# Half of a first MLP layer as seven Strassen block products, with token sums on GpSimd, in a fused window attention and MLP kernel

## The chip, the cores and the metric

One core of a Trainium2 chip runs the whole program; the other cores stay idle. The metric is device microseconds of one execution, the median of several runs; lower is better. Engines are named as in the profile: PE (TensorE, matmuls; PEld are its weight loads), DVE (VectorE), ACT (ScalarE), POOL (GpSimd), SP (SyncE, here a DMA queue).

## The reference

Attention over 4 batches, 8 heads, 768 tokens and 64 dimensions, where each query sees the last 128 tokens and the first 4; then a layer norm, an MLP of 512 to 2048 to 512 with ReLU, and a residual sum:

```python
scores = scale * np.matmul(q, k.transpose(0, 1, 3, 2))
keep = is_sink | in_window            # pos < 4, or 0 <= rel < 128
a = softmax(np.where(keep, scores, -1e9))
x = concat_heads(np.matmul(a, v))     # (4, 768, 512)
mu, var = mean(x), var(x)             # over the 512 features
xn = (x - mu) / np.sqrt(var + 1e-06) * g_ln
out = x + np.maximum(xn @ w_ch1, 0.0) @ w_ch2
```

## The kernel before

The 3072 tokens are 24 tiles of 128, taken two at a time: 12 chunks of 256 tokens, three per batch. All matmul operands are bf16, sums are fp32 in PSUM.

**Attention of a chunk** (`chunk`, `attend`, `value`). q and k are loaded by GpSimd's DMA queue into `nat` tiles (L659), transposed by DMA on SP's queue (L551) into `kq`; v goes into `vn` (L562). Scores are made in two halves (PE, L763, with four small matmuls for the sink tokens, L767), exponentiated on ScalarE (L777) and masked on VectorE (L781, two bf16 tensors in SBUF). For each of the two tiles, `value` multiplies with v (L800, L805) into a PSUM pair; VectorE takes the reciprocal of the row sum (L818), writes x (L820), its statistics (L824, L826); GpSimd takes the inverse root (L832, L833); VectorE writes the centred and scaled x (L835, `xc`), and SP transposes it by DMA into `xnt`, the right operand of the MLP.

**MLP of a chunk** (`mlp`, `wino`). The first layer is eight units of 8 matmuls of 256 columns (L880): unit u gives two of the 16 blocks of 128 hidden features, in one PSUM bank; ScalarE applies the ReLU on the way into `hq` (L890). From chunk 2 on the second layer is a Strassen product in Winograd's form (`wino`): VectorE makes eight sums of hidden blocks (`hs`, L943: s1 to s4, each for two halves g), PE makes seven products p1 to p7 of 8 matmuls of 256 columns (L960) in three banks, and VectorE drains them with the residual (`tm`, L974) and into the output tile (`ot`, L981). p6 adds onto p1's bank region after p1 was copied by L974, p4 and p5 onto others likewise. The sums of the weight blocks are made once (L1029). Chunks 0 and 1 make the first layer by tile, in matmuls of 128 columns (L873), and have a plain second layer (L911).

**What sets the order.** Nothing is issued in the order of the source. Every operation is registered in a `Plan` with a priority, the engines that may run it and a duration; `Plan.run` simulates the engines, picks the ready operation of the lowest priority number, and the program is emitted in that order; each engine then executes its own list strictly in that order. The attention of chunk c+1 (`value`) falls between the units of chunk c's MLP, and the scores of chunk c+2 between the second-layer products of chunk c. Buffers are taken from rings (`P.ring`) with a fixed number of slots; PSUM has two pairs (attention) and four single banks `one` (everything else). Priorities are 16 per chunk (`T`, `at`) plus offsets from the dictionary `PAR`.

Of the kernel before, what the change touches and what calls it, by code (L numbers as in the profile page):

```python
# [7 lines left out]
FP32 = mybir.dt.float32  # L8
BF16 = mybir.dt.bfloat16
AF = mybir.ActivationFunctionType  # L10
ALU = mybir.AluOpType
# [198 lines left out]


def fix(occ, extra=0.09):
    return (occ, occ + extra)
# [13 lines left out]
NEVER = -1e9  # L227

PAR = dict(split=(3, 4, 5, 6, 7), gsum=-8.0, guard=183.0, strict=40.0, win=0.4, tr=-8.0, sc=-5.3, sc1=-2.0, av=2.0, trx=9.0, by_dma=4, x_by_dma=2, g_on_w=2, av2=20.0, avi=1.0, behind=5, gtt=9.0, ramp=0.3, vs0=2.6, vpb=12.0,
           w1p=(0.15, 1.7, 2.05, 2.8), pm=2, w2p=(4.5, 4.51, 4.52, 4.53), by_tile=2, wino=2, vp=(0.0, 0.1, 2.0, 2.1, 4.2, 4.3), ld1=0.05)  # L230


def general(tc, nc, slots, pairs, ones, ident_f, ident, w1, w2, mhalf, g_s, g_r, q, k, v, out, scale):
# [128 lines left out]
def kernel(  # L362
# [34 lines left out]
    def ring(name, n, shape, dtype, pool=consts):  # L397
        P.ring(name, [Slot(pool.tile(shape, dtype, name=f"{name}{i}"), f"{name}{i}") for i in range(n)])
# [8 lines left out]
    ring("nat", 8, [128, H, 64], BF16)  # L407
    ring("vn", 7, [128, H, 65], BF16)
    ring("kq", 4, [128, HP, 2, 256], BF16)
    ring("pe", 12, [128, 2, 512], BF16)  # L410
    ring("ps", 3, [128, 256], BF16)
    ring("kts", 2, [128, HP, 32], BF16)
    ring("x", 16, [128, DM], BF16)
    ring("xc", 6, [128, DM], BF16)
    ring("xnt", 4, [128, NDM, 256], BF16)
    ring("hq", 8, [128, 4, 512], BF16)
    ring("hs", 10, [128, 2, 2, 128], BF16)
    ring("tm", 6, [128, 256], FP32)
    ring("ot", 4, [128, DM], FP32)
    ring("st", 16, [128, 24], FP32)  # L420
# [317 lines left out]
    def attend(c):  # L738
# [48 lines left out]
        for i in range(2):  # L787
            def part(h, n, i=i):
                col = 256 * i + 128 * n if R else 128 * (i + n)
                return pes[h // 2].t[:, h % 2, col:col + 128]  # L790
            value(c, i, pes, ps, (PAR["av2"] if c == 2 else at(c, "av")) + PAR["avi"] * i, part, [2 * c + i - 1, 2 * c + i] if R or i else [2 * c])

    def value(c, i, pes, ps, d, part, srcs):
        b, R, t = c // RC, c % RC, 2 * c + i
# [2 lines left out]
        def av(e):  # L797
# [5 lines left out]
            for h in range(H):  # L803
# [14 lines left out]
        P.op(f"rc{t}", {"DVE": fix(0.115)}, d + 0.1, lambda e: V.reciprocal(rc(), pv()[:, :, :, 64]),  # L818
             reads=[po], writes=[rcb])
        P.op(f"x{t}", {"DVE": dve(512)}, d + 0.11, lambda e: V.tensor_tensor(  # L820
            x.t.rearrange("p (a h c) -> p a h c", a=2, c=64), pv()[:, :, :, 0:64],
            rc().unsqueeze(3).to_broadcast([128, 2, 4, 64]), op=ALU.mult), reads=[po, rcb], writes=[x])
        mv = Buf(f"mv{t}")
        P.op(f"bn{t}", {"DVE": fix(0.60)}, d + 0.12, lambda e: V.bn_stats(st.t[:, 8:14], x.t),  # L824
             reads=[x], writes=[st, mv])
        P.op(f"ag{t}", {"DVE": fix(0.09)}, d + 0.13, lambda e: V.bn_aggr(st.t[:, 14:16], st.t[:, 8:14]),  # L826
             reads=[st], rw=[mv])
        rs = Buf(f"rs{t}")
        xst_b[t, "rs"] = rs
        scaled = c >= PAR["wino"]  # L830
        roots[t] = P.op(f"rs{t}", {"POOL": (0.83, 0.88)}, d + (0.5 if scaled else 5), lambda e: (
            G.tensor_scalar(st.t[:, 17:18], st.t[:, 15:16], 1e-6, None, op0=ALU.add),  # L832
            G.tensor_tensor(st.t[:, 16:17], st.t[:, 17:18], mhalf, op=ALU.pow)),  # L833
            reads=[st, mv, Bc["mhalf"]], writes=[rs])
        P.op(f"xc{t}", {"DVE": fix(0.26)}, d + (0.6 if scaled else 0.14), lambda e: V.tensor_scalar(  # L835
            xc.t, x.t, st.t[:, 14:15], st.t[:, 16:17] if scaled else None, op0=ALU.subtract,
            **({"op1": ALU.mult} if scaled else {})), reads=[x, st, mv] + ([rs] if scaled else []), writes=[xc])
        pt = Buf(f"ptx{t}", "one")
# [14 lines left out]
        if c >= PAR["g_on_w"]:  # L853
# [4 lines left out]
            [nc.scalar.mul(dst()[:, j], src()[:, j], gt[:, j:j + 1]) for j in range(NDM)]),  # L858
            reads=[pt, Bc["gt"]], writes=[xnt_b[c], xnt_t[t]])

    def mlp(c):
        T = 16.0 * c + 8.0
        xnt = xnt_b[c]
        h1 = []
        by_tile = c < PAR["by_tile"]
        hq = [Buf(f"hq{c}_{g}", "hq") for g in range(2)]
        for u in range(NH1 // 2):
            ph, hb, hg = Buf(f"ph{c}_{u}", "one"), Buf(f"h{c}_{u}"), hq[u // 4]

            def mm_t(e, u=u, ph=ph):  # L870
                for s in range(4):
                    for j in range(NDM):
                        nc.tensor.matmul(ph.t[:, 128 * s:128 * s + 128], lhsT=w1[u // 2][:, j, 128 * s:128 * s + 128],  # L873
                                         rhs=xnt.t[:, j, 128 * (u % 2):128 * (u % 2) + 128], start=j == 0, stop=j == NDM - 1)

            def mm(e, u=u, ph=ph):
                for s in range(2):
                    ht = 2 * u + s
                    for j in range(NDM):
                        nc.tensor.matmul(ph.t[:, 256 * s:256 * s + 256],  # L880
                                         lhsT=w1[ht // 4][:, j, 128 * (ht % 4):128 * (ht % 4 + 1)],
                                         rhs=xnt.t[:, j, :], start=j == 0, stop=j == NDM - 1)
            pr = T + u + 0.5
            o = P.op(f"ph{c}_{u}", pe(0.872), pr, mm_t if by_tile else mm, reads=[xnt_t[2 * c + u % 2] if by_tile else xnt, (Bw1 if c < PAR["g_on_w"] else Bw1g)[u // 2]],
                     writes=[ph], hold=[hb, hg, xnt])
            last_use[u // 2] = [o]

            def rl(e, ph=ph, hg=hg, u=u):
                if e == "ACT":
                    nc.scalar.activation(hg.t[:, u % 4, :], ph.t, AF.Relu)  # L890
                else:
                    V.tensor_scalar_max(hg.t[:, u % 4, :], ph.t, 0.0)
            P.op(f"rl{c}_{u}", {"ACT": act(512), "DVE": dve(512)}, pr - 3, rl, reads=[ph], writes=[hb], hold=[hg])
            h1.append(hb)
        T += 8
        if c >= PAR["wino"]:
            return wino(c, T, hq, h1)
        for i in range(2):
            t = 2 * c + i
            b, r = t // RB, t % RB  # L900
# [26 lines left out]
    def wino(c, T, hq, h1):  # L927
# [3 lines left out]
        deps = {n: [h1[4 * g + (0 if n[2] == "1" else 1)::2][:2] for g in range(2)] for n in part}  # L931
        sb = {}

        def get(n, g):
# [4 lines left out]
        for i, (n, x0, x1, op) in enumerate((("s3", "a11", "a21", ALU.subtract), ("s1", "a21", "a22", ALU.add),  # L939
                                             ("s2", "s1", "a11", ALU.subtract), ("s4", "a12", "s2", ALU.subtract))):  # L940
            for g in range(2):
                sb[n, g] = Buf(f"{n}_{c}{g}", "hs")
                P.op(f"{n}_{c}{g}", {"DVE": dve(512, 0.52)}, T - 4 + 4 * g + 0.2 * i, lambda e, n=n, x0=x0, x1=x1, g=g, op=op: V.tensor_tensor(  # L943
                    sb[n, g].t, get(x0, g), get(x1, g), op=op),
                    reads=need(x0, g) + need(x1, g), writes=[sb[n, g]], hold=[hq[g]])
        bank = {n: Buf(f"bk{n}{c}", "one") for n in "xyw"}
# [24 lines left out]
        def keep(name, r, done, half, pr):  # L971
            tm[name] = Buf(f"tm{name}{c}", "tm")
            i, sl = half // 2, slice(256 * (half % 2), 256 * (half % 2) + 256)
            return P.op(f"tm{name}_{c}", {"DVE": dve(256, 1.14)}, pr, lambda e: V.tensor_tensor(  # L974
                tm[name].t, at(r), xs[i].t[:, sl], op=ALU.add), reads=[done, xs[i]], hold=[bank[reg[r][0]]], writes=[tm[name]])
        oo = {}

        def final(r, done, name, half, pr):
            i, sl = half // 2, slice(256 * (half % 2), 256 * (half % 2) + 256)
            oo[half] = Buf(f"oo{c}{half}")  # L980
            return P.op(f"o{c}_{half}", {"DVE": dve(256, 1.14)}, pr, lambda e: V.tensor_tensor(  # L981
                ots[i].t[:, sl], at(r), tm[name].t, op=ALU.add), reads=[done, tm[name]], hold=[bank[reg[r][0]]], writes=[ots[i], oo[half]])

        lo, hi = slice(0, 256), slice(256, 512)
# [46 lines left out]
                writes=[Bw2t[i][qt]], after=idle[i])  # L1031

    for c in range(NC):
        mlp(c)
# [94 lines left out]
```

## Time and profile before

| | us |
|---|---|
| median of 3 runs | 211.26 |
| lowest and highest | 210.96, 211.36 |
| profiled execution, whole | 211.71 |
| its span, first to last instruction | 210.2 |
| busy PE, DVE, ACT, POOL in the span | 203.0, 162.2, 114.1, 83.5 |
| chunk periods (start of the first unit to the next chunk's), chunks 2 to 10 | 15.20, 15.87, 15.60, 15.20, 15.88, 15.60, 15.20, 15.88, 14.63 |
| chunk 11 to the end of the span | 16.45 |

The span is what the trace covers; 1.5 us of the execution lie around it. The pattern of three periods follows the attention that is mixed in: a chunk whose next chunk starts a batch has fewer value matmuls (15.20), a chunk whose next but one starts a batch has fewer score matmuls (15.60). A busy time of DVE or ACT is the union of instructions; neighbours on DVE overlap by 0.08 to 0.09 us in the trace, so a row's mean is longer than the room that an instruction takes in a full queue.

### The profile page before, as it was taken

To read this page: it belongs to the slowest core of one execution; us is meant where nothing else is said; L and a number is where in the kernel's file an instruction comes from. 1 tells how busy PE (TensorE), PEld (TensorE's weight loads), DVE (VectorE), ACT (ScalarE), POOL (GpSimd) and SP (SyncE) were. 2 spreads that over 40 slices of the span, in tenths; PEclk is the share of its full clock that TensorE was granted. 3 is DMA by queue.
4 is the path that set the end of the run, shared out by engine and by line. 5 is a ranking of instruction groups with operands and counts; after the bars stand their busy time and mean duration, and the time that the engine had idled before them with its cause. 6 is when DMAs were issued, how large, how long until landed. Compare 5 with 4: busy or idle time off the path is not lost.

```text
span 210.2 us, 6259 instructions
## 1 busy us (share of the span) xinstructions
PE 203.0 (97%) x2539; PEld 167.9 (80%) x2544; DVE 162.2 (77%) x410; ACT 114.1 (54%) x168; POOL 83.5 (40%) x126
## 2 busy tenths in 40 slices
PE   6978999999999999999999999999999999999994
PEld 2657997764787997997987987987988988988883
DVE  5579759999688688798687797797787786797353
ACT  2559479837564564564556555554457457450620
POOL 7967583369058057058066066066020020020000
PEclk9999999999999999999999999999999999999999
DMA  5999999999999949939959939939954520220202
GB/s 115 156 198 191 199 191 208 189 173 154 212 167 127 172 109 136 188 78 120 166 122 150 174 79 156 172 77 151 177 100 53 150 53 3 100 50 4 103 30 83
DMA packets 101243, 27.51 MB, mean 131 GB/s; under 512 B 89556, under 2 KB 99032, under 8 KB 101208
## 3 DMA queue, kind: packets, MB, share of 16 engines
q0 software_dynamic: 67712, 13.37, 77.7%
q1 hardware_dynamic: 33208, 13.41, 35.5%
q8 instruction: 21, 0.34, 0.7%
q10 hardware_dynamic: 288, 0.26, 0.4%
q14 instruction: 14, 0.11, 0.2%
HBM read 27.30 MB, written 6.29 MB: 160 GB/s over the span
## 4 chain that ended last, share of the span: by engine, by line
PE 90%; DMA 3%; DVE 3%; POOL 2%; issue 0%; DVEq 0%
PE one L880 33%; PE one L960 30%; PE one L873 7%; PE one L911 7%; PE pair L805 5%; PE pair L763 4%; DMA n4b<-in_q_dram 3%; PE pair L800 2%; PE one L645 1%; POOL nat L599 1%; PE one L767 1%; DVE xnt L857 1%; DVE kq L568 1%; POOL vn L562 0%; DVE st L824 0%
## 5 line engine op out<-in xcount | busy, mean ns | idle before, releaser
L890 ACT ACTIVATE hq<-one 128x512 bf16<-128x512 f32 x92 | 55.0, 597 | 55.7 <-PE one L880 46.7
L880 PE MATMUL one<-xnt,w 128*128 128x256 bf16 x640 | 74.5, 273 | 0.0
L880 PEld LDWEIGHTS <-w 128*128 128x128 bf16 x640 | 61.4, 98 | 7.0
L777 ACT ACTIVATE pe<-pair 128x1024 bf16<-128x1024 f32 (+1 forms) x40 | 36.2, 960 | 23.2 <-PE pair L763 19.0
L832 POOL TENSOR_SCALAR st<-st 128x1 f32<-128x1 f32 x24 | 6.2, 259 | 88.2 <-DVE rec L818 74.6
L960 PEld LDWEIGHTS <-hs 128*128 128x128 bf16 x320 | 30.0, 98 | 5.2 <-DVE tm L974 0.3
L974 DVE TENSOR_TENSOR tm<-one,x 128x256 f32<-128x256 f32 x40 | 16.9, 422 | 12.3 <-PE one L960 12.3
L781 DVE TENSOR_TENSOR pe<-pe,mask 128x1024 bf16<-128x1024 bf16 (+1 forms) x40 | 24.9, 644 | 1.0 <-ACT pe L777 0.8
L960 PEld LDWEIGHTS <-hq 128*128 128x128 bf16 x240 | 23.5, 98 | 2.7
L562 POOL DMA_DIRECT2D vn<-in_v_dram x24 | 21.8, 922 | 2.0 <-DMA w<-in_moe_w_ch_dram 1.1
L943 DVE TENSOR_TENSOR hs<-hq 128x512 bf16<-128x512 bf16 x40 | 15.4, 413 | 5.3 <-ACT hq L890 5.2
L960 PE MATMUL one<-w,hq 128*128 128x256 bf16 x160 | 19.1, 273 | 0.0
L981 DVE TENSOR_TENSOR ot<-one,tm 128x256 f32<-128x256 f32 x40 | 16.7, 418 | 1.1 <-PE one L960 0.9
L820 DVE TENSOR_TENSOR x<-pair,rec 128x512 bf16<-128x512 f32 x24 | 16.6, 691 | 0.8
L824 DVE BATCH_NORM_STATS2 st<-x 128x6 f32<-128x512 bf16 x24 | 16.6, 692 | 0.5
L873 PE MATMUL one<-xnt,w 128*128 128x128 bf16 x256 | 16.3, 219 | 0.5 <-DVE xnt L857 0.5
L873 PEld LDWEIGHTS <-w 128*128 128x128 bf16 x256 | 14.7, 98 | 1.6 <-issue 0.5
L659 POOL DMA_DIRECT2D nat<-in_k_dram x16 | 15.0, 938 | 2.5 <-DMA w<-in_moe_w_ch_dram 2.5
L659 POOL DMA_DIRECT2D nat<-in_q_dram x16 | 14.2, 898 | 3.4 <-DMA w<-in_moe_w_ch_dram 3.4
L833 POOL TENSOR_TENSOR st<-st,mhalf 128x1 f32<-128x1 f32 x24 | 14.2, 592 | 2.0
L911 PE MATMUL one<-w,hq 128*128 128x512 bf16 x60 | 14.8, 380 | 0.2
L805 PE MATMUL pair<-vn,pe 128*128 128x65 bf16 x352 | 14.6, 193 | 0.0
(113 smaller groups left out, 245.1 us busy)
## 6 DMA issues: line engine op xcount, KB each, us to landing
out_dram<-ot SPq DMA_DIRECT2D x17, 256.0 KB
w<-in_moe_w_ch_dram POOLq DMA_DIRECT2D x8, 512.0 KB, 12.6
vn<-in_v_dram POOLq DMA_DIRECT2D x24, 128.0 KB, 7.2
nat<-in_k_dram POOLq DMA_DIRECT2D x17, 128.0 KB, 4.8
nat<-in_q_dram POOLq DMA_DIRECT2D x17, 128.0 KB, 5.3
out_dram<-ot SPq DMA_DIRECT2D x14, 128.0 KB
kq<-nat SPq DMA_TRANSPOSE x32
xnt<-xc SPq DMA_TRANSPOSE x20
```

The lines of the kernel that those rows point to most:

```text
L562: P.op(f"vld{t}", {"POOL": (0.87, 0.9)}, prio, lambda e: G.dma_start(bv.t[:, :, 0:64], v[b, :, 128 * r:128 * (r + 1), :].rearrange("h p d ...
L659: lambda e, nat=nat, ap=ap: G.dma_start(nat.t, ap), writes=[nat], dma=SW, after=behind(c))
L777: P.op(f"ex{c}{hp}", {"ACT": act(2 * n)}, d + 0.1 + 0.05 * j, lambda e, pp=pp, pb=pb: nc.scalar.activation(pb.t[:, :, 0:n], pp.t[:, :, 0:n ...
L781: V.tensor_mul(pb.t[:, :, 0:n], pb.t[:, :, 0:n], mm),
L805: nc.tensor.matmul(po.t[:, h // 4, 65 * (h % 4):65 * (h % 4) + 65], lhsT=part(h, n), rhs=vn_b[tv].t[:, h, :], start=(not R and h % 4 == 0 ...
L873: nc.tensor.matmul(ph.t[:, 128 * s:128 * s + 128], lhsT=w1[u // 2][:, j, 128 * s:128 * s + 128], rhs=xnt.t[:, j, 128 * (u % 2):128 * (u % ...
L880: nc.tensor.matmul(ph.t[:, 256 * s:256 * s + 256], lhsT=w1[ht // 4][:, j, 128 * (ht % 4):128 * (ht % 4 + 1)], rhs=xnt.t[:, j, :], start=j ...
L890: nc.scalar.activation(hg.t[:, u % 4, :], ph.t, AF.Relu)
L911: nc.tensor.matmul(pc.t[:, 0:wd], lhsT=(hq[s // 2].t[:, (2 * s + i) % 4, 128 * ii:128 * ii + 128] if by_tile else hq[ht // 8].t[:, ht // 2 ...
L960: nc.tensor.matmul(at(r), lhsT=get(left, g)[:, v, s, :], rhs=rhs, start=first and n == 0, stop=n == 7, skip_group_check=True)
L974: return P.op(f"tm{name}_{c}", {"DVE": dve(256, 1.14)}, pr, lambda e: V.tensor_tensor(tm[name].t, at(r), xs[i].t[:, sl], op=ALU.add), read ...
L981: return P.op(f"o{c}_{half}", {"DVE": dve(256, 1.14)}, pr, lambda e: V.tensor_tensor(ots[i].t[:, sl], at(r), tm[name].t, op=ALU.add), read ...
```

## The change

From chunk 4 on (`half=4`), units 0 to 3 of the first layer, which are hidden features 0 to 1023 (weight tiles `w1[0]` and `w1[1]`), are no longer made by L880 but by `halves`: a 2 x 2 x 2 block product (two halves of the hidden features, of the 512 inputs and of the 256 tokens) in Winograd's form with seven products m1 to m7. Each is 8 matmuls of 128 columns into a whole bank. GpSimd makes four differences t0 to t3 of token halves of `xnt` per chunk, VectorE makes four sums of weight blocks once. m1, m6, m7 and m4 follow each other on bank z, m5 and m3 on bank y, m2 on bank w. ScalarE copies m1, m5 and (m1+m6) from PSUM into fp32 tiles `tz`; VectorE adds a bank and a copy into the raw blocks c11, c12, c22; ScalarE applies the ReLU to these in place, and to c21 straight from PSUM. Units 4 to 7 are as before. In the built order one chunk of PE reads: m1, the p3 of the chunk before, m5, m2, value of tile one, m6, unit 5, m3, value of tile two, m7, units 4 and 6, m4, unit 7, p1, scores, p2, p7, p6, scores, p4, p5.

For chunks above 4 the attention's priorities come from a second dictionary, and the second layer's sums get new ones. In the built order VectorE thereby does the reciprocal, x and statistics of both tiles ahead of the second layer's sums; q and k loads stand about a chunk later, with the q loads behind the token sums. Rings shrink: `nat` 8 to 6, `pe` 12 to 10, `x` 16 to 12, `xc` 6 to 5; `xt` (2) and `tz` (3) are new, and the weight sums keep two `hq` slots.

```diff
 PAR = dict(...
+           h=dict(av=1.72, avi=0.98, sc=-6.42, sc1=-3.15, tr=9.57, trx=9.0, xo=-18.83), tzp=4.09, kp=0.16, half=4, wsum=58.0, flip=1, te=("POOL",), tlead=4.51, rd=0, cpr=22.05, sp=(28.86, 6.78), sq=(-4.01, -21.74, -2.19, 9.73), pos=(-1.32, 1.36, 2.64, 4.31, -0.61, 2.25, 2.96), pos4=(3.22, 2.48, 3.68, 8.36))
...
-        return 16.0 * c - 8.0 + PAR[step]
+        return 16.0 * c - 8.0 + (PAR["h"] if c > PAR["half"] else PAR)[step]
...
+    def weight_sums():
+        a = [w1[m][:, 2 * i:2 * i + 2, :] for m in range(2) for i in range(2)]
...
+        for i, (x0, x1, op) in enumerate((("a21", "a22", ALU.add), (0, "a11", ALU.subtract),
+                                          ("a11", "a21", ALU.subtract), ("a12", 1, ALU.subtract))):
...
+                 V.tensor_tensor(ap(), val(x0), val(x1), op=op), ...
+    def halves(c, T, hq):
...
+        B = {f"b{i + 1}{j + 1}": (lambda i=i, o=128 * (j ^ f): xnt.t[:, 2 * i:2 * i + 2, o:o + 128]) for i in range(2) for j in range(2)}
...
+        for i, (n, x0, x1) in enumerate((("t0", "b12", "b11"), ("t2", "b22", "b12"), ("t1", "b22", "t0"), ("t3", "b21", "t1"))):
...
+            P.op(f"xt{n}_{c}", ..., lambda e, ...: (V if e == "DVE" else G).tensor_tensor(
+                right(n), right(x0), right(x1), op=ALU.subtract), ...
+        def product(i, bank, left, rt, first, after=()):
...
+                for h in range(4):
+                    for kk in range(2):
+                        nc.tensor.matmul(b.t[:, 128 * h:128 * h + 128], lhsT=lt[:, kk, 128 * h:128 * h + 128], rhs=rh[:, kk, :],
+                                         start=first and h == 0 and kk == 0, stop=kk == 1, skip_group_check=True)
...
+        def snap(i, bank, done):
...
+            o = P.op(f"tz{i}_{c}", {"ACT": act(512)}, ..., lambda e: nc.scalar.copy(tz.t, banks_[bank].t), ...
+        def total(n, bank, done, tz, pr):
...
+            o = P.op(f"c{n}_{c}", {"DVE": dve(512, 1.14)}, pr, lambda e: V.tensor_tensor(
+                block(n), banks_[bank].t.rearrange("p (i t) -> p i t", i=4), tz.t.rearrange("p (i t) -> p i t", i=4), op=ALU.add), ...
+            P.op(f"r{n}_{c}", ..., lambda e: nc.scalar.activation(block(n), block(n), AF.Relu) ...
+        m1 = product(1, "z", "a11", "b11", True)
+        t1, o1 = snap(1, "z", m1)
+        m5 = product(5, "y", 0, "t0", True)
+        t5, o5 = snap(5, "y", m5)
+        m2 = product(2, "w", "a12", "b21", True)
+        total("c11", "w", m2, t1, T + pos[1] - late_)
+        m6 = product(6, "z", 1, "t1", False, [o1])
+        t2, o2 = snap(6, "z", m6)
+        m3 = product(3, "y", 3, "b22", False, [o5])
+        total("c12", "y", m3, t2, T + pos[5] - late_)
+        m7 = product(7, "z", 2, "t2", False, [o2])
+        o3 = total("c22", "z", m7, t5, T + pos[6] - late_)
+        m4 = product(4, "z", "a22", "t3", False, [o3])
...
+        P.op(f"rc21_{c}", {"ACT": act(512)}, ..., lambda e: nc.scalar.activation(
+            block("c21"), banks_["z"].t.rearrange("p (i t) -> p i t", i=4), AF.Relu), ...
...
-        for u in range(NH1 // 2):
+        strassen = c >= PAR["half"]
+        quick = halves(c, T, hq[0]) if strassen else None
+        for u in range(4 if strassen else 0, NH1 // 2):
```

More of the change, by code (lines that the diff above doesn't have):

```diff
@@ L830, in value @@
         scaled = c >= PAR["wino"]
-        roots[t] = P.op(f"rs{t}", {"POOL": (0.83, 0.88)}, d + (0.5 if scaled else 5), lambda e: (
+        roots[t] = P.op(f"rs{t}", {"POOL": (0.83, 0.88)}, d + xo + (0.5 if scaled else 5), lambda e: (
             G.tensor_scalar(st.t[:, 17:18], st.t[:, 15:16], 1e-6, None, op0=ALU.add),
@@ L859, in value @@
             reads=[pt, Bc["gt"]], writes=[xnt_b[c], xnt_t[t]])
+    wsum, xt_b = [], {}
+    def weight_sums():
+        a = [w1[m][:, 2 * i:2 * i + 2, :] for m in range(2) for i in range(2)]
+        get = {n: (lambda i=i: a[i]) for i, n in enumerate(("a11", "a12", "a21", "a22"))}
+        held = [Buf(f"ws{i}", "hq") for i in range(2)]
+        for i, (x0, x1, op) in enumerate((("a21", "a22", ALU.add), (0, "a11", ALU.subtract),
+                                          ("a11", "a21", ALU.subtract), ("a12", 1, ALU.subtract))):
+            done = Buf(f"wsum{i}")
+            ap = lambda i=i: held[i // 2].t[:, 2 * (i % 2):2 * (i % 2) + 2, :]
+            val = lambda x: ap(x) if isinstance(x, int) else get[x]()
+            P.op(f"wsum{i}", {"DVE": dve(1024, 0.52)}, PAR["wsum"] + 3.0 * i, lambda e, ap=ap, x0=x0, x1=x1, op=op, val=val:
+                 V.tensor_tensor(ap(), val(x0), val(x1), op=op), reads=Bw1g[0:2] + [wsum[x][1] for x in (x0, x1) if isinstance(x, int)],
+                 hold=[held[i // 2]], writes=[done], nb=PAR["wsum"] + 3.0 * i)
+            wsum.append((ap, done, held[i // 2]))
@@ L930, in wino @@
                 "a12": lambda g: A[g]()[:, 1, :, :, 0:128], "a22": lambda g: A[g]()[:, 1, :, :, 128:256]}
-        deps = {n: [h1[4 * g + (0 if n[2] == "1" else 1)::2][:2] for g in range(2)] for n in part}
+        if quick:
+            h1 = [None] * 4 + h1
+        deps = {n: [quick[int(n[1]) - 1] if quick and g == 0 else h1[4 * g + (0 if n[2] == "1" else 1)::2][:2] for g in range(2)] for n in part}
         sb = {}
@@ L980, in final @@
             oo[half] = Buf(f"oo{c}{half}")
-            return P.op(f"o{c}_{half}", {"DVE": dve(256, 1.14)}, pr, lambda e: V.tensor_tensor(
+            return P.op(f"o{c}_{half}", {"DVE": dve(256, 1.14)}, pr - PAR["kp"], lambda e: V.tensor_tensor(
                 ots[i].t[:, sl], at(r), tm[name].t, op=ALU.add), reads=[done, tm[name]], hold=[bank[reg[r][0]]], writes=[ots[i], oo[half]])
@@ L1033 @@
     for c in range(NC):
+        if c == PAR["half"]:
+            weight_sums()
         mlp(c)
```

79 lines of the change are left out of this document (63 added, 16 removed).

## The prediction

> **What bounds the kernel now.** I read the page's shares first, then the chain that ended last, then that chain in order of time, then busy time chunk by chunk. Page, busy shares and chain:
>
> ```profile
> PE 203.0 (97%) x2539; PEld 167.9 (80%) x2544; DVE 162.2 (77%) x410; ACT 114.1 (54%) x168; POOL 83.5 (40%) x126
> ...
> PE 90%; DMA 3%; DVE 3%; POOL 2%; issue 0%; DVEq 0%
> PE one L880 33%; PE one L960 30%; PE one L873 7%; PE one L911 7%; PE pair L805 5%; PE pair L763 4%; DMA n4b<-in_q_dram 3%; PE pair L800 2%; PE one L645 1%; POOL nat L599 1%; PE one L767 1%; DVE xnt L857 1%; DVE kq L568 1%; POOL vn L562 0%; DVE st L824 0%
> ```
>
> TensorE is the chain, and a third of it is the line that the change rewrites (L880). In order of time (start, length), one piece from the early chunks and then chunk 9:
>
> ```profile
> 22.64 0.89 PE one L873 x16
> ...
> 163.24 1.75 PE one L880 x16
> 164.99 0.22 PE pair L800 x2
> 165.21 0.48 PE pair L805 x16
> 165.70 0.87 PE one L880 x8
> ...
> 167.28 4.37 PE one L880 x40
> 171.64 1.75 PE one L960 x16
> ```
>
> No piece of "issue" stands between them: PE has no gap that could swallow a saving. A 256-column matmul costs 1.75/16 = 109 ns, a 128-column one 0.89/16 = 55.6 ns, each with a weight load of its own. The chunks, engine by engine (4 and 9):
>
> ```profile
> core 0: us, PE busy (x) PEld busy (x) DVE busy (x) ACT busy (x) POOL busy (x), PEclk, DMA share, GB/s
> 85.76:101.36 15.60, 15.60 (x175) 13.47 (x173) 12.92 (x33) 7.80 (x12) 7.02 (x10) 1.00 1.33 132
> 163.24:179.12 15.88, 15.88 (x211) 13.79 (x209) 12.26 (x31) 8.93 (x13) 1.69 (x4) 1.00 0.26 68
> ```
>
> VectorE has only 2.7 us free in chunk 4: second in line, and it gets new work. Granted clock is 1.00 throughout.
>
> **The change, part by part.**
>
> *Products on PE.* Removed in each of chunks 4 to 11: units 0 to 3, 32 x 109 ns = 3.49 us. Added: seven products of 8 matmuls of 128 columns, 56 x 55.6 ns = 3.11 us. Difference 0.38 us per chunk, **3.0 us** in eight. All of it is on the path.
>
> A rule of the Trainium skill speaks against this: "TensorE: Matmul & The Clock Gate", section "Back-to-back issue gap", gives about 81 ns for a sustained 128-column matmul with its weight load. By it the 56 would take 4.54 us and the kernel would lose 8.3 us; the row above, 55.6 ns, does not agree.
>
> *VectorE.* Groups used for prices:
>
> ```profile
> L890 ACT ACTIVATE hq<-one 128x512 bf16<-128x512 f32 x92 | 55.0, 597 | 55.7 <-PE one L880 46.7 <-PE one L873 8.6 <-DVE st L826 0.4
> L974 DVE TENSOR_TENSOR tm<-one,x 128x256 f32<-128x256 f32 x40 | 16.9, 422 | 12.3 <-PE one L960 12.3
> L943 DVE TENSOR_TENSOR hs<-hq 128x512 bf16<-128x512 bf16 x40 | 15.4, 413 | 5.3 <-ACT hq L890 5.2
> L919 DVE SCALAR_TENSOR_TENSOR ot<-one,st,x 128x512 f32<-128x512 f32 x4 | 3.0, 740 | 0.0
> L463 POOL TENSOR_SCALAR_AFFINE_SELECT upper<-upper 128x128 bf16<-128x128 bf16 x1 | 0.3, 294 | 0.0
> ```
>
> Three additions of a 512-wide PSUM bank and an fp32 copy per chunk. Nearest row L919, 740 ns; neighbours overlap by 0.08 to 0.09 us in the timeline (an L974 of 0.42 is followed 0.33 later), so 0.65 each, 1.95 per chunk; ends 0.42 (L974, half the width) and 0.74. Chunk 4 goes from 12.92 to 14.87 us of a period of 15.60 - 0.38 = 15.22: only 0.35 free. Four weight sums of 1024 elements (0.6 each by the masks of L781) run once in chunks 2 and 3, where VectorE has about 3 us free per chunk: 0, at most 0.5 if each delays a copy that PE wants.
>
> *ScalarE.* Four ReLUs go; three bank copies, three ReLUs in SBUF and one ReLU from PSUM come: 7 - 4 = 3 at 0.6 = 1.8 us, so 8.9 becomes 10.7 of 15.5. Room enough; what matters is the queue order, below.
>
> *GpSimd.* Four subtractions of 256 bf16 elements per chunk. No such row: below it L463 (half the elements, one input) 0.29; above it the two-input L833 (0.59 for one element) plus two L463, 1.18. I take 0.7, between. They wait for both input transposes and stand in the queue behind the two root pairs and four loads of 0.93 us, and two q loads and the next roots are behind them.
>
> **Walk of one chunk** (9, built order, 0 = first product m1; 0.2 us from a last matmul to its reader as L960 to L974 shows, 0.1 us back to PE). PE: m1 0, second-layer p3 of the chunk before 0.45, m5 1.32, m2 1.76, attention 2.21, m6 2.91, unit 5 3.36, m3 4.23, attention 4.67, m7 5.38, unit 4 5.82, unit 6 6.69, m4 7.57, unit 7 8.01, p1 8.88, scores, p2 10.44, p7 11.31, p6 12.18, scores, p4 13.5, p5 14.4.
> - m6 writes on m1's bank: ScalarE copies it 0.65 to 1.25; m6 is due at 2.91. Hidden.
> - m7 writes on m6's: the copy stands behind the ReLU of c11 (addition 2.60 to 3.30, ReLU 3.35 to 3.95), so 3.9 to 4.5; due 5.38. Slack 0.8.
> - m4 clears the bank when c22 is added, 6.0 to 6.7; due 7.57. Slack 0.75.
> - GpSimd: roots until 9.65, loads until 13.4, then t0, t2, t1, t3 done at 14.1, 14.8, 15.5, 16.2; the next chunk wants t0 at 16.8, t1 at 18.4. Hidden at both ends: with 1.18 each, t1 is done at 16.9.
> - VectorE: the second addition pushes the statistics, so the second tile's centred x is written at 10.3 to 10.6, not 8 as before, and eight second-layer sums and the copy of p1 (L974) end at 11.7. p6 may start at 11.8; due 12.18. Slack 0.4: the narrowest place.
>
> With the other chunks' own queues this place turns late: chunks 5 and 8, whose attention has fewer matmuls (period 0.7 shorter, VectorE's list the same), p6 due 11.53, ready 11.86: 0.33 each; chunk 10 has no scores before p2: 0.28; chunk 11: 0.1. Sum given back **1.0 us**.
>
> *Order, smaller pools, stores* (nat 8 to 6, pe 12 to 10, x 16 to 12, xc 6 to 5; loads about a chunk later). q loads wait on GpSimd for the transposes of the chunk before and hold the next roots; I get them off the queue about 3.6 us into the chunk, the roots are asked at 5.7. Cost 0; if 2 us later, each microsecond beyond goes to VectorE.
>
> **Sum:** 3.0 - 1.0 = 2.0 us. The profiled execution took 211.71 (span 210.2), so 209.7 there; the median of the runs lies 0.45 lower, 211.26, which gives **209.3**.
>
> **Rivals.**
> 1. *VectorE becomes the bound (slower).* Its sums and masks read two SBUF tensors, and GpSimd now reads two as well. If they hold each other up, of the 12 such operations per chunk three or four meet the 2.8 us of token sums and wait half a sum, 1.2 us in all; beyond the 0.6 us that is free, 0.6 per chunk reaches PE, in seven chunks 4.2 us: 213.5. It decides from 0.3 us per chunk on. For it: little is free. Against it: sums at 123.1 to 125.3 keep 0.42 us although GpSimd's L832 and L833 run from 123.26 to 124.25 (those read one element). The stretch where they meet is followed by 0.7 us of VectorE's slack before c11. The Trainium skill ("SBUF — State Buffer", "Who interferes with whom") says just this: such a VectorE instruction and a GpSimd instruction that reads SBUF exclude each other for a whole instruction. No run here shows it yet.
> 2. *The handoffs eat it (no change).* PE to ScalarE to PE three times on one bank, with the bank's reader queued behind others: 0.25 us more per chunk than walked, 211.3. For: slacks of 0.4 to 0.8. Against: ScalarE is a third idle.
> 3. *Weight loads set the pace.* At the row's 98 ns per load not hidden, 56 x 98 = 5.5 us: 2.0 worse per chunk, 227. Against: L873's 55.6. By the Trainium skill's 81 ns it would be 219.6.
> 4. *All slack holds:* the full 3.0, 208.2.
>
> **Numbers.** Forecast with rival 4 (208 to 210.5) 0.64; rival 2 0.10; rival 1 0.24; rival 3 0.02. Within 0.2% (0.4 us, about what a measurement of this kernel can tell) only rival 2's middle, 0.08, its edges going to faster (0.01) and slower (0.01). Faster 0.65, same 0.08, slower 0.27. Range 207.9 to 213.6: from the full gain with a little over, to rival 1's price.
>
> **What would show it.** Right: the new product line at 55 to 57 ns per matmul, chunk periods near 15.5, 15.1 and 15.2 instead of 15.88, 15.20 and 15.60, VectorE above 90% in chunks 4 to 10, small PE waits on L974's successor only. Wrong: PE idle before products released by GpSimd or ScalarE; masks or sums longer than 0.68 and 0.42 us where token sums run; token sums over 1.6 us each.

## The result and the profile after

Slower: 219.34 us, median of 4 runs (217.18 to 220.97), against 211.31 in the kernel before on the same chip (210.96 to 211.44); ratio 1.035, 95% interval 1.027 to 1.042. Medians here and below are of all runs, while ratios leave out a run that lies more than 1.5% above the fastest of its kernel (here 220.97). The forecast was 209.3. The profiled execution took 217.18, its span 215.7, 5.5 more than before's 210.2. Busy shares and the chain, from the page:

```profile
PE 201.8 (94%) x2731; PEld 167.9 (78%) x2736; DVE 180.1 (84%) x440; ACT 124.2 (58%) x190; POOL 108.0 (50%) x158
...
PE 27%; DMA 2%; DVE 1%; issue 0%
PE one L1059 12%; PE one L977 6%; PE one L908 6%; DMA xnt<-xc 2%; PE pair L808 1%; PE pair L766 1%; PE pair L803 0%; PE one L770 0%; DVE ot L1080 0%; DVE tm L1073 0%; DVE hs L1042 0%; PE one L1156 0%; PE one L1150 0%
```

TensorE is busy 1.2 us less than before, but its share fell from 97% to 94%: it waits. The chain could be followed back only to 147 us, so its shares add up to 30%. The transposition of x (`DMA xnt<-xc`), absent from the chain before, stands in it. (L1059 is the second layer's products, L977 the old units, L908 the new products, L1073 and L1080 VectorE's copies.) From the list of waits (waiter, releaser: us, times, longest):

```profile
POOL nat L662 <- DMA kq<-nat: 21.5, 7, 9.5
...
DVE xc L839 <- POOL st L837: 3.7, 4, 2.0
...
PE one L908 <- DMA xnt<-xc: 2.8, 3, 1.8
...
PE one L1059 <- DVE tm L1073: 2.7, 3, 1.1
```

Read from the bottom: TensorE waits for VectorE's copies and for transposed x; VectorE waits for GpSimd's roots; GpSimd waits with its q loads (L662) for transposes that free a `nat` tile. Before, TensorE had none of these waits. By stage, against the period before less the 0.38 us that the products save (p3 of the chunk before, 0.87 us, now stands behind the m1 that starts a chunk, which is allowed for in chunks 3 and 11; chunk 10 before is taken as 14.73, to its first unit at 193.68, where 14.63 ended at the small L1049 matmuls ahead of it): chunk 2 is 2.6 us longer, chunk 3 0.9, chunk 5 2.0, chunk 7 1.2, chunk 8 0.7, the other chunks 0.6 together, and 1.6 more pass between the last matmul and the end of the span; chunk 2 starts 0.9 earlier. Together, before rounding, 8.6, less the 3.0 saved: the 5.5 of the span, to 0.1.

Two places in the timeline. Chunk 2, GpSimd, then VectorE (start, length, instruction, in brackets the idle time and its releaser):

```profile
59.29 1.76 POOL L662 DMA_DIRECT2D nat<-in_q_dram  x2 [9.48 <-DMA kq<-nat]
61.12 0.22 POOL L836 TENSOR_SCALAR st<-st 128x1 f32<-128x1 f32 x1
61.43 0.57 POOL L837 TENSOR_TENSOR st<-st,mhalf 128x1 f32<-128x1 f32 x1
```

```profile
59.62 0.42 DVE L1042 TENSOR_TENSOR hs<-hq,hs 128x512 bf16<-128x512 bf16 x1
62.03 0.41 DVE L839 TENSOR_SCALAR xc<-x,st 128x512 bf16<-128x512 bf16 x1 [1.99 <-POOL st L837]
```

The two q loads hold GpSimd for 9.5 us; the root behind them, whose statistics are aggregated by 57.93, starts at 61.12, and VectorE stands still for it. TensorE then waits 1.05 us for p6's bank and 0.75 for p4's; one weight sum (0.66 us at 63.18) is also ahead of the first copy and another (0.69 at 66.70) ahead of p4's. Chunk 5: VectorE, SyncE, TensorE.

```profile
110.34 0.69 DVE L828 BATCH_NORM_STATS2 st<-x 128x6 f32<-128x512 bf16 x1
111.00 0.76 DVE L1042 TENSOR_TENSOR hs<-hq 128x512 bf16<-128x512 bf16 x2
111.68 0.42 DVE L1042 TENSOR_TENSOR hs<-hs,hq 128x512 bf16<-128x512 bf16 x1
112.01 0.42 DVE L1042 TENSOR_TENSOR hs<-hq 128x512 bf16<-128x512 bf16 x1
112.35 0.17 DVE L830 BATCH_NORM_AGGREGATE st<-st 128x2 f32<-128x6 f32 x1
...
113.63 0.41 DVE L839 TENSOR_SCALAR xc<-x,st 128x512 bf16<-128x512 bf16 x1
```

```profile
110.45 4.82 SPq L554 DMA_TRANSPOSE xnt<-xc  x2
```

```profile
119.58 0.61 PE L908 MATMUL one<-xnt,w 128*128 128x128 bf16 x8 [1.79 <-DMA xnt<-xc]
```

Four second-layer sums (L1042) stand between a tile's statistics and their 0.17 us aggregation, so the root and the centred x come late; the transposition is issued by 115.27 (110.45 + 4.82) and lands 4.3 us later, and m1 waits 1.79 us.

### The profile page after: what moved, and what is told of

Same layout as the page of the kernel before. It is cut to its first block, busy times and chain, and to the rows that moved or that the text cites. A ratio compares the mean times of both kernels' runs of the same rounds, so it can differ in the third digit from the quotient of the medians.

```text
span 215.7 us, 6713 instructions
## 1 busy us (share of the span) xinstructions
PE 201.8 (94%) x2731; PEld 167.9 (78%) x2736; DVE 180.1 (84%) x440; ACT 124.2 (58%) x190; POOL 108.0 (50%) x158
## 5 line engine op out<-in xcount | busy, mean ns | idle before, releaser
L977 PE MATMUL one<-xnt,w 128*128 128x256 bf16 x384 | 46.8, 273 | 0.3 <-DMA xnt<-xc 0.3
L987 ACT ACTIVATE hq<-one 128x512 bf16<-128x512 f32 x58 | 33.8, 595 | 20.6 <-PE one L977 10.8
L977 PEld LDWEIGHTS <-w 128*128 128x128 bf16 x384 | 36.3, 98 | 4.5 <-issue 0.5
L1059 PEld LDWEIGHTS <-hs 128*128 128x128 bf16 x320 | 30.8, 98 | 6.4 <-issue 2.7
L784 DVE TENSOR_TENSOR pe<-pe,mask 128x1024 bf16<-128x1024 bf16 (+1 forms) x40 | 26.9, 678 | 1.3 <-ACT pe L780 1.1
L662 POOL DMA_DIRECT2D nat<-in_q_dram x16 | 14.3, 898 | 25.0 <-DMA kq<-nat 21.5
L1059 PEld LDWEIGHTS <-hq 128*128 128x128 bf16 x240 | 22.3, 98 | 5.0 <-issue 1.6
L919 ACT COPY tz<-one 128x512 f32<-128x512 f32 x24 | 13.9, 580 | 20.2 <-PE one L908 14.0
L892 POOL TENSOR_TENSOR xt<-xnt 128x256 bf16<-128x256 bf16 x16 | 12.8, 818 | 23.3 <-DMA xnt<-xc 23.3
L933 ACT ACTIVATE hq<-hq 128x512 bf16<-128x512 bf16 x24 | 15.1, 630 | 12.3 <-DVE hq L930 12.3
L1080 DVE TENSOR_TENSOR ot<-one,tm 128x256 f32<-128x256 f32 x40 | 16.8, 419 | 5.7 <-PE one L1059 4.8
L1059 PE MATMUL one<-w,hq 128*128 128x256 bf16 x160 | 20.3, 273 | 0.0
L930 DVE TENSOR_TENSOR hq<-one,tz 128x512 bf16<-128x512 f32 x24 | 16.3, 689 | 4.2 <-PE one L908 4.2
L1073 DVE TENSOR_TENSOR tm<-one,x 128x256 f32<-128x256 f32 x40 | 16.7, 418 | 0.7 <-PE one L1059 0.4
L1042 DVE TENSOR_TENSOR hs<-hq 128x512 bf16<-128x512 bf16 x40 | 15.5, 416 | 1.7 <-ACT hq L987 1.5
L908 PEld LDWEIGHTS <-hq 128*128 128x128 bf16 x256 | 15.9, 98 | 0.4
```

What stands on the lines that cost most here:

```text
L784: V.tensor_mul(pb.t[:, :, 0:n], pb.t[:, :, 0:n], mm),
L908: nc.tensor.matmul(b.t[:, 128 * h:128 * h + 128], lhsT=lt[:, kk, 128 * h:128 * h + 128], rhs=rh[:, kk, :], start=first and h == 0 and kk = ...
L977: nc.tensor.matmul(ph.t[:, 256 * s:256 * s + 256], lhsT=w1[ht // 4][:, j, 128 * (ht % 4):128 * (ht % 4 + 1)], rhs=xnt.t[:, j, :], start=j ...
L1059: nc.tensor.matmul(at(r), lhsT=get(left, g)[:, v, s, :], rhs=rhs, start=first and n == 0, stop=n == 7, skip_group_check=True)
L1073: return P.op(f"tm{name}_{c}", {"DVE": dve(256, 1.14)}, pr - PAR["kp"], lambda e: V.tensor_tensor(tm[name].t, at(r), xs[i].t[:, sl], op=AL ...
L1080: return P.op(f"o{c}_{half}", {"DVE": dve(256, 1.14)}, pr - PAR["kp"], lambda e: V.tensor_tensor(ots[i].t[:, sl], at(r), tm[name].t, op=AL ...
```

## The experiments

Medians and ratios to the kernel before on the same chip; "last" is where the last matmul starts in the profiled span (before: 207.47), "end" what follows to the end of the span (before: 2.7).

| kernel | median, us | ratio, 95% interval | last | end |
|---|---|---|---|---|
| changed kernel | 219.34 | 1.035 (1.027 to 1.042) | 211.45 | 4.2 |
| e1 old x | 221.19 | 1.051 (1.044 to 1.059) | 214.72 | 4.3 |
| e2 no token sums | 219.22 | 1.037 (1.030 to 1.044) | 214.30 | 4.2 |
| e3 q loads of chunk 5 later | 219.08 | 1.038 (1.035 to 1.041) | 210.77 | 4.3 |
| e4 and weight sums moved | 218.27 | 1.033 (1.027 to 1.038) | 212.68 | 4.3 |
| e5 and roots first | 215.53 | 1.017 (1.013 to 1.021) | 209.57 | 4.5 |
| e6 e5, no token sums | 215.40 | 1.022 (1.016 to 1.028) | 209.04 | 4.2 |
| e7 e1, no token sums | 217.94 | 1.033 (1.029 to 1.037) | 211.10 | 4.3 |
| e8 no products | 214.56 | 1.014 (1.012 to 1.017) | 211.97 | 2.7 |
| e9 e5 and statistics early | 212.28 | 1.004 (1.001 to 1.007) | 205.88 | 4.2 |
| e10 e5 and loads early | 221.41 | 1.045 (1.038 to 1.052) | 216.82 | 4.3 |
| e11 e9 and e10 | 216.49 | 1.023 (1.020 to 1.027) | 210.65 | 4.4 |
| e12 e11, no fallback | 215.81 | 1.017 (1.011 to 1.023) | | |
| e13, e14, e15 e9 with padding | 212.38, 212.42, 212.49 | 1.005, 1.006, 1.006 | 205.8 to 206.8 | 4.2 to 4.4 |
| e16 e9, no token sums | 211.82 | 1.003 (0.999 to 1.006) | 205.27 | 4.4 |
| e17 e9, all chunks | 211.26 | 1.001 (0.998 to 1.004) | 205.18 | 4.4 |
| e18 e17, no fallback | 210.14 | 0.994 (0.992 to 0.996) | 207.30 | 2.6 |

Moves change one engine's list at a time and leave every other list as it is; only in e8 the planner makes a new order.

### Is it the wait for x, or the token sums? (e1, e2, e7)

```diff
 e1, e7: units, products and token sums of chunk c >= 4
-    xnt = xnt_b[c]
+    xnt = xnt_b[c - 1]
 e2, e7: token sums
-    G.tensor_tensor(right(n), right(x0), right(x1), op=ALU.subtract)     # and right("t0") = a block of x
```

> Instruction lists as in the changed kernel (profiled span 215.7, time 217.2); from chunk 4 on, the first layer and the token sums read the transposed x of the chunk before, so that no product waits for a transposition that has just been issued (the output is that of other data; all instructions are still there). Theory 'late x': the waits of m1 for xnt (0.7 before chunk 4, 1.8 before chunk 6, 0.3 before chunk 9) and part of the 1.2 us of chunk 7 go, 3 us: about 214. Rival 'contention' (token sums hold up VectorE): the waits come from VectorE and stay, 217. Rival 'more VectorE work': less than 1 us, 216.5.

> The four subtractions on GpSimd of each chunk are left out; m5, m6, m7 and m4 read token blocks of x instead (another result, the same matmuls, same order elsewhere). Rival 'contention': masks go from 714 back to 683 ns, 2 us of VectorE come back and 1.5 to 2 us of time: 215.5. Theory 'late x': m1 still waits for xnt as before, at most 0.5 us: 216.7 to 217.2. If the sums on GpSimd hold PE directly (t0 after m1), 0.5 to 1 more.

> e1_old_x (MLP of the chunk before's x, no wait for x transposes) without the token sums on GpSimd. In e1 VectorE was busy 186.2 us against 180.1 and its p6 waits summed to 4.9 us. Rival 'contention': without GpSimd's sums VectorE falls by 6 to 8 us to 178, the waits go, 4 to 5 us less than e1: 216.5. If the 1.3 to 1.4 us waits of VectorE for GpSimd's roots do it: no more than 1.5 us less, 219.7.

e1 refuted "late x" as I had stated it: with m1's waits gone it is slower still, 221.2. TensorE ran ahead until VectorE held it: p6 now waits 0.88, 1.23, 1.01 and 1.80 us. e2 gained nothing either, since m1 went on waiting (2.25 us ahead of chunk 6). With both away (e7) the time is 3.3 us below e1, but only 1.4 below the changed kernel, and the two ratios overlap: in e7 VectorE still waits 8.0 us for GpSimd's roots, and p6 0.79, 1.05 and 0.98 us in three chunks. What the token sums do to a full VectorE is in the groups of e1, then of e7 (line, operation, shape, count, busy us, mean ns):

```profile
L784 DVE TENSOR_TENSOR pe<-pe,mask 128x1024 bf16<-128x1024 bf16 x28 | 20.5, 737 | 0.5 <-ACT pe L780 0.5
...
L1043 DVE TENSOR_TENSOR hs<-hq,hs 128x512 bf16<-128x512 bf16 x20 | 10.9, 545 | 0.1
L1043 DVE TENSOR_TENSOR hs<-hs,hq 128x512 bf16<-128x512 bf16 x20 | 10.3, 513 | 0.1
```

```profile
L784 DVE TENSOR_TENSOR pe<-pe,mask 128x1024 bf16<-128x1024 bf16 x28 | 18.9, 682 | 0.1
...
L1042 DVE TENSOR_TENSOR hs<-hs,hq 128x512 bf16<-128x512 bf16 x20 | 8.4, 419 | 0.1
L1042 DVE TENSOR_TENSOR hs<-hq,hs 128x512 bf16<-128x512 bf16 x20 | 8.3, 414 | 0.1
```

The same sums take 513 and 545 ns beside GpSimd's and 419 and 414 without; all of VectorE is busy 186.2 us against 177.6. The contention of rival 1 is real. The Trainium skill ("SBUF — State Buffer", "Who interferes with whom") names just these: VectorE instructions with two SBUF inputs against GpSimd instructions that read SBUF; the rows agree. How much of it there is depends on what meets the token sums: from chunk 4 on 11 masks of 1024 elements and 12 sums run beside them in e1, but only 6 and one in the changed kernel, whose masks went from 683 to 714 ns. VectorE's copies out of PSUM (L1073, L1080), with one SBUF input, keep their 417 ns beside the token sums (24 of them in the changed kernel; 419 elsewhere). Removing one wait alone gained nothing, since another was next in line.

### GpSimd's list (e3, e4, e5, e6) and the order without products (e8)

```diff
 GpSimd, chunk 2 (e3) and each chunk from 3 on (e5)
-  q load, q load                      (wait for transposes: nat has 6 tiles)
   L836, L837: root of the first tile
+  q load, q load                      (e3: behind both roots)
   L836, L837: root of the second tile
 VectorE (e4, and e5 with it)
-  four weight sums, 3 us apart, among the copies of chunk 2 and at its end
+  two ahead of tile 6's reciprocal, two ahead of tile 8's, where VectorE idles
 e8, the whole kernel
-        strassen = c >= PAR["half"]
+        strassen = False                # and no weight_sums()
```

> One edit of GpSimd's list: the two q loads of chunk 5 stand behind the inverse roots of tiles 6 and 7 instead of ahead of them (in the changed kernel they wait 9.5 us for transposes to free two nat tiles). Theory 'queue': the roots of tile 6 start 2.4 us earlier, the 1.99 us wait of xc goes, p6 of chunk 2 no longer waits 1.05 us: 1.0 to 1.9 us less, about 215.7, chunk 2 about 16.2 instead of 17.8. Rival: the weight sums alone make chunk 2 late: under 0.4 us.

> As e3_q_loads_later, and the four weight sums on VectorE stand where it idles (two ahead of the statistics of tile 6, two ahead of those of tile 8) instead of between the copies and sums of chunk 2. Theory 'queue': p4's 0.75 us goes as well, chunk 2 at 15.3 instead of 17.8: 2.4 us less than the changed kernel, about 214.8. Rival 'contention' and rival 'more VectorE work from chunk 4 on': under 0.5 us, 216.7, as both act later.

> e4_q_and_weight_sums plus one more edit of GpSimd's list: in every later chunk the two q loads stand behind the inverse root of the first tile, not ahead of it (in e4 they wait 1 to 2.6 us there for transposes to free a nat tile, and VectorE then waits 1.8 us at 94.9 and 1.4 us at 144.2 for the root). Theory 'queue': those waits go, the centred x of both tiles and its transposes are 1 to 1.5 us earlier in chunks 4 to 8, the 1.04 and 0.98 us waits of p6 and half of m1's 1.96 us go: 2.5 us less than e4, profiled span about 214.5, time about 215.7. Rival 'VectorE and GpSimd hold each other': VectorE is full with or without it, the waits of p6 stay, less than 0.7 us.

> e5_roots_first without the token sums on GpSimd (m5, m6, m7 and m4 read token blocks of x instead; another result, same matmuls). Rival 'contention': once the queue no longer holds VectorE, its slower masks and sums (2 us of 27 in the changed kernel, 6 us in e1) are what is left: 2 us or more below e5. Theory 'queue': within 0.7 us of e5.

> The change without its products: units 0 to 3 as before, no token or weight sums, no additions; the smaller rings, the second set of attention priorities and the new order of the second layer's sums stay. If rings and order alone cost time: 213 to 214 with p6 or xnt waits in the trace. If the products' own work is what makes the queues late: 211.2 to 211.7, no waits of PE over 0.3 us.

e3 and e4 do what they should in place: chunk 2's waits of 1.05 and 0.75 us are gone. But the total hardly moves (1.035 to 1.033): TensorE arrives earlier at chunk 4 and p6 waits 1.04 us there, because such loads hold roots in later chunks too (in e4 VectorE waits 1.8 us at 94.9 and 1.4 at 144.2 for one). In e4's profiled execution x also came 1.11 us late for chunk 3. e5 takes the loads away from ahead of the first root everywhere: 2.7 us less than e4, 3.8 less than the changed kernel. With the lists in this order e6 shows no cost of the token sums that is clear of noise: the medians of e5 and e6 are 0.13 apart and their intervals overlap. e8 is the plainest: smaller rings and new priorities **without any product** already cost 1.4%, 3.1 us, with 7.5 us of VectorE waiting for GpSimd's roots. So a loss of more than a third of the 8.0 us needs no product. Rings and priorities were not tried apart, and e8's order is the planner's own, so this is not a share of the changed kernel's loss.

### VectorE's list and the landing of x (e9, e10, e11, e16)

```diff
 VectorE, second tile, chunk 5 (e9; likewise 4 to 10)
   L828 statistics
+  L830 aggregation
   hs, hs, hs
+  L839 centred x
   hs
-  L830 aggregation
   hs, hs, hs
-  L839 centred x
 GpSimd (e10)
-  root, q, q, root, k, k, v, v | token sums of the next chunk
+  root, root, q, q             | token sums of the next chunk, k, k, v, v
```

> e5_roots_first with one edit of VectorE's list: from chunk 4 on the small aggregation of the statistics stands right behind the statistics (in e5 four second-layer sums stand between them in chunk 5, 1.4 us), and the second tile's centred x three sums behind it. Theory 'late x': that x is written 0.7 us earlier in chunks 4, 6, 7 and 1.4 in 5 and 8, so its transposes land earlier; of e5's waits of m1 (1.11, 1.94, 0.55) 2.5 us go, the sums behind it cost p6 at most 0.3 in two chunks: 2 us less than e5, 213.4. If the landing is held by other transfers and not by the time of issue, less than 0.7 us.

> e5_roots_first with one edit of GpSimd's list: from chunk 4 on the two k and two v loads stand behind the token sums of the next chunk, and the q loads behind both roots, so that fewer loads run beside the transposes of x. In e5 these land 4.05 and 4.55 us after the end of their issue in chunks 4 and 5, 3.15 to 3.5 later on, and 1.38 in chunks 9 and 10, where neither loads nor q and k transposes run. Theory 'transfers in the way': 3.0 us instead, 1 to 1.5 us less of each m1 wait: 2 us less than e5, 213.5. Rival 'issue time alone': the same landing, within 0.5 us of e5; if the loads now come too late for their transposes, slower.

> Both edits, e9_stats_early and e10_loads_early. Theory: no wait of m1 is left above 0.2 us, the span is e5's 214.0 less 3.6: 210.4, time 211.9; what remains against the predicted 209.3 is the end (4.4 us from the last product's successor to the end of the span, 2.7 before) and some p6. Rival: VectorE takes the place of the transposes, p6 waits 0.5 us in four chunks: 213.5.

> e9_stats_early without the token sums on GpSimd (m5, m6, m7 and m4 read token blocks of x; another result, same matmuls). Rival 'contention': VectorE is busy 181.6 us in e9; it falls by 3 us or more, and the time by 0.5 to 0.8 (e9's waits of 0.79 us in all are what can go). If contention costs no time any more: within 0.3 us of e9.

e9 gave about 3 us more than e5 (3.3 by the medians, 2.7 by the ratios), beyond the 2 expected, by 0.1 us of work moved forward by 1.4 us and the centred x moved with it; m1's waits of 1.11 and 1.94 us in e5 became 0.33 and none. In chunk 5 the second centred x is written 9.8 us after m1 instead of 11.3. e10 failed: the loads ahead of the roots held VectorE again (0.5 to 1.0 us in five chunks), the q loads took the place of the k and v loads beside the transposes, and x landed 3.3 to 5.0 us after issue; 221.4. e11 shows the same harm on top of e9. Whether fewer transfers beside it would make x land sooner these two therefore do not tell: loads moved along a queue that also carries the roots do other harm first. e16: without token sums 0.46 us less than e9 by the medians, with intervals that overlap: whether contention still costs time in the mended order cannot be told from noise.

### The end of the program (e12 to e15, e17, e18)

```diff
 e13, e14, e15: inside the fallback branch, which is not taken
+    17 small copies on ScalarE | 81 small writes on VectorE | 32 small matmuls on TensorE
 e12 (on e11), e18 (on e17): the body of that branch
-    general(tc, nc, slots, pairs, ...)
+    nc.vector.memset(n_bad, 0.0)
 e17 (on e9), VectorE, tiles 6 to 9
-  statistics, sum, aggregation, reciprocal, x, sum, sum, sum, xc, statistics, aggregation, sum, sum, sum, xc
+  statistics, aggregation, sum, reciprocal, x, xc, statistics, aggregation, sum, sum, xc, sum, sum, sum, sum
```

> e11_both without the body of the fallback branch at the end of the program (it is not taken for these inputs; a single small write stands in its place). In all kernels with the products 4.3 us lie between the last small matmul and the end of the span, and one more instruction load runs there 1 us before the end, against 2.7 us in the kernel before and in e8_no_products. Theory 'instruction loads at the jump': the end shrinks by 1.5 us or more against e11. If it is the output stores: no difference.

> e9_stats_early with 17 small copies on ScalarE inside the fallback branch, which is not taken: nothing that runs changes, only the place of the end of ScalarE's program (475 instructions before, 492 now, as in the kernel before the change). If ScalarE's instruction loads make the end longer, the 4.2 us from the last small matmul to the end of the span fall to 2.7 and the time by 1.5 us against e9; otherwise 4.2 and e9's 212.3.

> The same with 81 small writes on VectorE inside the fallback branch (708 instructions to 789). If VectorE's instruction loads make the end longer: 2.7 us at the end instead of 4.2, time 210.8. Otherwise as e9.

> The same with 32 small matmuls on TensorE inside the fallback branch (7530 instructions to 7658). If TensorE's instruction loads make the end longer: 2.7 us at the end instead of 4.2, time 210.8. Otherwise as e9.

> e9_stats_early with the same edit of VectorE's list in chunks 2 and 3 (tiles 6 to 9: statistics and aggregation ahead of the second layer's sums, the centred x of the second tile two sums behind). Theory 'late x': the waits of 0.4 to 0.9 us before chunk 3 and 0.2 to 0.5 before chunk 4 go; 0.6 to 0.9 us less than e9: 211.5, level with the kernel before within 0.3%; TensorE's last matmul at about 205 us of the span, 2.4 earlier than before, the end still 4.2 us. Rival: the sums come too late in chunk 2 and p6 waits instead, as e9.

> e17_all_chunks without the body of the fallback branch (not taken for these inputs). If the longer end is instruction loading for the jump over that body: no instruction load after the last matmul, 1.5 us less than e17, 210.0. If it only moves from the span to what lies around it: the span is 1.5 shorter and the time within 0.5 us of e17.

e17 leaves TensorE 0.75 us of waits over 0.15 from chunk 2 to the last product, and its last matmul starts at 205.18, 2.3 us earlier than before; 0.5 of that lies ahead of chunk 2, whose start scatters from 53.6 to 54.9 over the kernels, so 1.75 us is the gain from there on. The median is 1.0 below e9's, with intervals that overlap. Chunks 5 to 9 of e17:

```profile
core 0: us, PE busy (x) PEld busy (x) DVE busy (x) ACT busy (x) POOL busy (x), PEclk, DMA share, GB/s
100.09:114.92 14.83, 14.83 (x221) 13.16 (x221) 14.01 (x34) 10.08 (x16) 10.09 (x14) 1.00 1.40 136
114.92:130.42 15.50, 15.50 (x234) 13.77 (x232) 14.78 (x35) 10.35 (x17) 11.02 (x15) 1.00 1.48 141
130.42:145.66 15.24, 15.24 (x199) 13.47 (x197) 14.54 (x35) 9.27 (x16) 10.31 (x15) 1.00 1.61 135
145.66:160.49 14.83, 14.83 (x223) 13.16 (x220) 14.35 (x35) 10.08 (x16) 8.84 (x13) 1.00 1.14 136
160.49:176.00 15.51, 15.51 (x235) 13.76 (x233) 14.88 (x35) 10.36 (x17) 5.89 (x10) 1.00 0.27 70
```

PE busy equals the period in each, and the periods are those before (15.20, 15.88, 15.60) less 0.36 to 0.38: the saving that the prediction computed. VectorE is at 94 to 97%. Still e17 is level with the kernel before (1.001), because 1.7 us are lost after the last matmul. The DMA queues in that stretch, in the kernel before and in the changed kernel (packets, MB, share):

```profile
q1 hardware_dynamic: 288, 0.26, 28.5%
q8 instruction: 1, 0.02, 3.2%
q14 instruction: 2, 0.02, 2.0%
```

```profile
q1 hardware_dynamic: 288, 0.26, 18.4%
q8 instruction: 1, 0.02, 2.0%
q14 instruction: 3, 0.02, 1.8%
```

The stores are the same; one more instruction load runs, 0.5 us before the end. In e18 none runs there, the end is 2.6 us, and the time falls by 1.1 us, to 0.6% below the kernel before (the median span falls by 1.5, and 0.3 of it comes back outside the span). The Trainium skill ("Runtime: NRT & Kernel Launch", "Instruction fetch mechanics") says that a taken branch to a place outside the fetched window waits for a load of that place; e18 agrees in kind. But the kernel before jumps over the same body, has three loads in that stretch and ends as soon as e18 does (2.7), so a jump with loads does not by itself make the end long. Why the longer program needs one load more, and whether that load is what costs the time, is open: padding ScalarE, VectorE or TensorE (e13 to e15) left the end at 4.2 to 4.4. e12 had only shown 0.7 us against e11, within their intervals; e18 against e17, in more runs, is clear. e18 lacks the fallback and the kernel before was not run without its own, so it says what the end costs, not that the change pays.

## Why the prediction was wrong, step by step

- **Products on PE, 3.0 us: right.** Eight 128-column matmuls take 0.44 to 0.45 us, 0.38 per chunk shows in five periods of e17. Rival 3 (weight loads set the pace) is refuted; that the 219.6 named beside it lies close to the measured 219.34 is chance.
- **VectorE, three additions of 0.65: right.** L930 has a mean of 689 ns, 0.6 without the overlap. That VectorE would stand above 90% holds in chunks 5 to 9 of e17.
- **Token sums on GpSimd at 0.7 us: right** (mean 0.74 to 0.82, median 0.67 in the changed kernel).
- **Weight sums, 0 to 0.5: not refuted.** One stands ahead of p4's copy, which waited 0.75 us, but in e3, where the sums stay in place, that wait is gone with the q loads. Beyond e3, e4 moves them alone; the 0.8 us between the two medians is within their scatter.
- **Walk of a chunk: failed at "the second tile's centred x is written at 10.3 to 10.6".** The time was right (10.25 to 10.66 in chunk 9 of the changed kernel, 10.9 to 11.3 in chunk 5), but the walk stopped there. It asked whether p6's sums are late and not when that x, transposed, reaches m1. The landing, 4.3 us after issue beside other transfers, was not in the sum; before, x was written 2.4 (chunk 9) to 3.4 us (chunk 5) earlier in its chunk and TensorE never waited for it. GpSimd's "loads until 13.4, then t0" took the transposes as landed. e9 and e17, which move x and its statistics forward on VectorE's list and nothing else, recover 3.3 and 1.0 us by the medians (e17's 1.0 is not clear of noise, and acts in chunks 2 and 3, which have no products).
- **"Order, smaller pools, stores: cost 0": failed, with 3.8 us of the 8.0 (changed kernel to e5, the move of the weight sums included).** I placed the end of the q loads 3.6 us into the chunk and the roots at 5.7. The q loads wait in GpSimd's queue for a `nat` tile (9.5, 6.4, then 0.3 to 1.7 us) and leave it 7.4 us into chunk 2, where the root was asked at 4.3, and 7.0 into chunk 7, asked at 5.7; in chunks 3 to 6 they were off in time or within 0.1 us of it. The text named this price ("if 2 us later, each microsecond beyond goes to VectorE") and gave it no weight. e5 puts it at 2.7 us beyond e4; e8 puts rings and priorities without products at 3.1. Whether eight `nat` tiles instead of six would have done the same as the moves was not tried.
- **Given back at p6, 1.0 us:** in the mended kernel 0.25, in chunk 10 (forecast 0.28); chunks 5 and 8 give back nothing.
- **Rival 1 (slower by contention), 213.5:** the mechanism exists (e1 against e7: 3.3 us), the outcome came by another road: once GpSimd's list is in order, e6 and e16 show no difference clear of noise (0.13 and 0.46 us by the medians). **Rival 2 (handoffs between ScalarE and TensorE)** shows in no wait.
- **Not thought of: the end,** 1.6 (changed kernel) to 1.7 us (e17) longer after the last matmul.

Net: the gain on TensorE (1.75 us from chunk 2 to the last matmul in e17, where 2.0 was forecast) was real. It stood behind 8.1 us, which the order within two engines' lists alone took away (219.34 to 211.26), and the longer end takes what is left of it.

## What to carry to other kernels

When a change adds work to an engine that is second in line, follow each value of its list to the DMA it feeds and to the reader at the far side, with the landing time measured under load: the slack is at the end of that chain and not at the engine. A load that waits for a buffer holds everything behind it in its queue, so count what stands behind it before a ring is made smaller. And take out a small head of a long chain (0.1 us of aggregation) before cutting work. A wait that is taken away can come back at the next reader (e1, e2, e4), so a repair is judged by the whole chain and not by the wait that it removes.

## What the runs showed of the hardware

- **TensorE's granted clock fell to half after waits of 2.25 and 2.44 us, and not after 1.79 to 2.01.** In e2 m1 waited 2.25 us, to 120.75:

```profile
118.00:120.00 2.00, 0.50 (x5) 0.30 (x4) 2.00 (x5) 0.47 (x1) 0.00 (x0) 1.00 2.40 63
120.00:121.00 1.00, 0.25 (x5) 0.25 (x5) 0.01 (x1) 0.00 (x0) 0.00 (x0) 1.00 2.02 195
121.00:122.00 1.00, 1.00 (x14) 0.88 (x12) 0.00 (x0) 0.57 (x1) 0.00 (x0) 0.87 1.93 177
122.00:123.00 1.00, 1.00 (x10) 0.87 (x8) 0.40 (x1) 0.02 (x1) 0.00 (x0) 0.50 2.20 165
...
125.00:126.00 1.00, 1.00 (x22) 0.98 (x20) 0.54 (x3) 0.69 (x2) 1.00 (x2) 0.92 1.09 359
```

  The third column from the end is the granted clock: 1.00 until after the wait, then 0.50 for some 3.4 us, and PE is "busy" all the while. That chunk took 17.12 us instead of 15.50: the wait of 2.25 cost another 1.6. The same followed 2.44 us in e10; 1.79 to 2.01 us (the profiled executions of the changed kernel, e3, e4, e5, e6) were followed by no fall. Two falls do not give a limit. The Trainium skill ("TensorE: Matmul & The Clock Gate", "Part 1: The HAM clock gate (the "warmup" mystery)") has the half clock after an idle window of about 3.4 us; here less was enough.
- **A transposition by DMA reaches its first reader 1.38 us after the end of its issue when nothing else moves** (chunks 9 and 10 in the changed kernel, e5 and e9). In chunks 3 to 7, where q, k and v loads run beside it, it takes 3.0 to 5.5 us; that the loads are the reason was not shown by a run. Chunk 9 of the changed kernel, SyncE and GpSimd (178.84 to 180.21):

```profile
174.12 4.72 SPq L554 DMA_TRANSPOSE xnt<-xc  x2
```

```profile
180.21 1.79 POOL L892 TENSOR_TENSOR xt<-xnt 128x256 bf16<-128x256 bf16 x2 [3.50 <-DMA xnt<-xc]
```

  Chunk 8, with q and k transposes issued right behind it and no loads, has 2.9 in the changed kernel and 3.2 in e5, but 1.4 to 1.5 in e9 and e17; what makes that difference stays open. In e18 one landing of 5.48 us made m1 wait 1.42, with lists that in e17 left no wait over 0.5: such landings are the likeliest source of the scatter from run to run (217.2 to 221.0 in the changed kernel, 211.0 to 211.4 before), which was not tried by itself.
- **The body of a branch that never runs cost 1.1 us** (e18 against e17), after all work was done; in the kernel before, with the same body, the end is as short as in e18.
